# When ten weight chunks are loaded and decoded beside the first block of the feed-forward

## The chip, the cores and the metric

The kernel runs on one core of one Trainium2 chip. Its time is the device time of one execution in microseconds (us); the time of a kernel is the median of the runs shown. A profile is one more execution, recorded by the hardware. Five engines work side by side, each through its own queue in order: TensorE (PE, with its weight loads PEld), VectorE (DVE), ScalarE (ACT), GpSimd (POOL) and SyncE (SP), which here issues all transfers between memory and the chip's buffers.

## The reference

```python
attn = 1.0 / (1.0 + np.exp(-(scale * q @ k.T - log(S))))     # sigmoid attention, per batch and head
x = (attn @ v), heads side by side                           # 3584 tokens x 768
h = x @ w_in                                                 # 768 x 2048
g = h * np.clip(h + 3.0, 0.0, 6.0) / 6.0
out = g @ w_out                                              # 2048 x 768
```

There are 8 batches, 12 heads, 448 positions and 64 numbers a head. The host hands w_in and w_out to the kernel as 64-bit floats, seen there as pairs of 32-bit words.

## The kernel before, in words

The 12 heads of a batch go in 6 pairs, so there are 48 pairs; the 3584 tokens go in 7 tiles of 512. The work has three stages. In the first, pairs 0 to 17 (batches 0 to 2) go through attention on raw inputs (`scores_native`, `av_native`). In the second, the other 30 pairs go through attention on operands split in a high and a low part, mixed with the first half of the feed-forward (`moe_in`) of earlier tiles, that of the last tile behind it; its results g are stored to memory (`gd`). In the third, w_out is applied (`moe_out`).

Between the first and the second stage stands a stretch of pure feed-forward, and the change is there. `moe_in(0)` makes the first token tile: 16 feature blocks of 18 products (L375) each. A block collects in one of two PSUM buffers named ph. When its 18 products are done, ACT (L379) and DVE (L380) turn it into g and so free the buffer; SP then stores g (L382). There are two buffers for g too.

The products need w_in as pairs of a high and a low part in SBUF. It comes in 32 half chunks, numbered n = 0 to 31 and called chunks here; chunks 2k and 2k+1 make the weights of block k. `load_wi(n)` handles one in three parts:

- the load: SP issues a transfer of 384 KB (L362) into a staging buffer;
- the decode (`join_f64`, L58 to L68): one ACT operation (L58), five on DVE (L59, L60, L61, L64, L65), one on POOL (L68, the add);
- the split (`split_f32`): one ACT operation (L73, the high part) and one on POOL (L74, the low part).

The staging buffers are borrowed. From n = 15 on, a chunk with n % 3 = 2 (20, 23, 26, 29) uses one single buffer, called wis here, which is also the buffer into which the q and k of a later pair are loaded (`qkr`, L165). It is free only after the split. The other chunks use two pairs of buffers (wiqh for the raw words, wiql for the result): the raw one is free after the decode on DVE, the other after the split.

`feed(part, i)` calls the parts by a clock of units i. In the first stage a unit is two steps of attention, and units run from 0 to 32. After that a unit is KU products of `moe_in(0)`: unit 33 begins at product 0, unit 34 at product KU, and so on. The list `first` holds the unit of each chunk's load; decode and split follow a fixed number of units later. In a unit, all loads are called first, then decodes, then splits. At product 160 the loads of pair 18 are called (L429), at product 224 its preparation (`prep`, from L181 on), and after 276 products the second stage begins.

In this part the order of instructions on PE, ACT, DVE and POOL is the order of the calls, written out by hand. The order on SP is set by a scheduler from its own estimate of times.

## Time and profile before

| | us |
|---|---|
| median of 3 runs | 1244.57 (1244.23 to 1244.61) |
| profiled execution | 1244.73 |
| its span, first to last instruction | 1242.7 |
| PE busy | 1220.3 |
| DVE busy | 724.2 |
| ACT busy | 519.5 |
| POOL busy | 256.5 |

The first stage ends on PE at 116.13 us from the start of the span, where the first product of `moe_in(0)` begins. The first scores of the second stage begin at 188.78, and the third stage's products at 781.7.

A timeline row reads: start and duration in us, engine, line of the kernel, operation, output<-inputs, the number of instructions merged in the row, and in brackets how long the engine had been idle before it and whose end it waited for. A row of the waits reads: who waited for whom, us in total, how often, the longest. A row of the windows reads: the stretch, its length, busy time and number of instructions of PE, PEld, DVE, ACT and POOL, the granted clock of PE as a share of full speed, the busy share of the transfer engines, and GB/s. A row of a source or tile view gives the shortest, median and longest duration in ns, and the first and last start in us.

### The profile page before, as it was taken

Reading aid. Unit: us, or ns where it says so; the run is one execution under the profiler, and the core shown is the slowest. Engines: PE = TensorE matmul, PEld = TensorE weight load, DVE = VectorE, ACT = ScalarE, POOL = GpSimd, SP = SyncE. Lnnn points to the kernel's source line nnn. Section 1 sums busy time; section 2 is a strip of 40 time slices with the busy share of each in tenths; the row PEclk is TensorE's granted clock in tenths of the full one; section 3 lists DMA queues with packets and bytes.
Section 4 is the critical chain, followed back from the end, with each engine's and each line's share of the span. In section 5 each row is a group of like instructions: output and inputs, shape, how many; then the busy total and the mean of one; then the engine's idle time right before and its main releaser. Section 6 shows DMA issues by size and latency. Waiting matters only on the chain.

```text
span 1242.7 us, 15076 instructions
## 1 busy us (share of the span) xinstructions
PE 1220.3 (98%) x5508; PEld 962.1 (77%) x5508; DVE 724.2 (58%) x1284; ACT 519.5 (42%) x671; POOL 256.5 (21%) x297
## 2 busy tenths in 40 slices
PE   8999699999999999999999999999999999999998
PEld 2334487888888888888888888888888888888887
DVE  4566458888888888988888589873030303030300
ACT  6775234666556665665656535322020202020200
POOL 3343343333333433433333000000000000000000
PEclk9999799999999999999999999999999999999999
DMA  7653335334443334433342177734040404040000
GB/s 248 192 169 113 111 114 155 107 93 113 117 111 107 92 113 117 117 110 89 107 117 80 50 220 285 247 105 152 26 161 26 161 26 161 18 161 26 26 26 25
DMA packets 62570, 142.68 MB, mean 115 GB/s; under 512 B 8224, under 2 KB 29728, under 8 KB 58912
## 3 DMA queue, kind: packets, MB, share of 16 engines
q1 hardware_dynamic: 62496, 141.72, 35.9%
q8 instruction: 43, 0.70, 0.2%
q14 instruction: 31, 0.25, 0.1%
HBM read 101.32 MB, written 40.37 MB: 114 GB/s over the span
## 4 chain that ended last, share of the span: by engine, by line
PE 88%; DVE 1%; issue 1%; POOL 0%; ACT 0%; DVEq 0%; POOLq 0%; ACTq 0%
PE po L539 37%; PE ph L375 36%; PE pv L327 6%; PE sc L270 3%; PE sc L271 3%; PE sc L267 1%; PE sc L314 1%; DVE vbh L191 0%; DVE ql L182 0%; DVE g L380 0%; DVE kbl L204 0%; DVE qp L205 0%; DVE al L277 0%; POOL wis L68 0%; POOL wi L74 0%
## 5 line engine op out<-in xcount | busy, mean ns | idle before, releaser
L375 PE MATMUL ph<-x,wi 128*128 128x512 f32 x2016 | 493.5, 395 | 13.1 <-DVE g L380 13.1
L375 PEld LDWEIGHTS ph<-x,wi 128*128 128x128 f32 x2016 | 379.5, 188 | 95.4 <-DVE g L380 14.3
L539 PE MATMUL po<-gl,woh 128*128 128x512 f32 x672 | 261.4, 389 | 0.0
L539 PE MATMUL po<-gh,woh 128*128 128x512 f32 x672 | 261.4, 389 | 0.0
L539 PE MATMUL po<-gh,wol 128*128 128x512 f32 x672 | 261.4, 389 | 0.0
L546 DVE TENSOR_SCALAR o<-po 128x512 f32<-128x512 f32 x42 | 29.0, 689 | 296.5 <-PE po L539 296.5
L499 ACT CAST gh<-gr 128x2048 fp32r<-128x2048 f32 x28 | 53.6, 1914 | 300.6 <-PE po L539 296.4
L277 DVE TENSOR_TENSOR al<-a,ah 128x896 fp32r<-128x896 f32 x120 | 141.1, 1176 | 50.8 <-ACT a L276 49.8
L539 PEld LDWEIGHTS po<-gh,wol 128*128 128x128 f32 x672 | 126.1, 188 | 26.3
L539 PEld LDWEIGHTS po<-gh,woh 128*128 128x128 f32 x672 | 126.1, 188 | 26.2
L539 PEld LDWEIGHTS po<-gl,woh 128*128 128x128 f32 x672 | 126.1, 188 | 26.1
L275 ACT ACTIVATE ah<-sc,bias_s 128x896 fp32r<-128x896 f32 x120 | 109.9, 915 | 74.6 <-PE sc L271 38.5
L178 POOL TENSOR_TENSOR ka<-qkr,ka 64x448 fp32r<-64x448 f32 x60 | 91.9, 1531 | 132.0 <-issue 118.7
L379 ACT ACTIVATE g<-ph,bias 128x512 f32<-128x512 f32 x112 | 77.2, 690 | 93.6 <-PE ph L375 85.0
L276 ACT ACTIVATE a<-sc,bias_s 128x896 f32<-128x896 f32 x120 | 109.2, 910 | 1.6 <-DVE al L277 0.7
L380 DVE SCALAR_TENSOR_TENSOR g<-g,ph 128x512 f32<-128x512 f32 x112 | 76.2, 680 | 31.6 <-ACT g L379 31.2
L500 DVE TENSOR_TENSOR gl<-gr,gh 128x2048 fp32r<-128x2048 f32 x28 | 64.1, 2289 | 29.1 <-ACT gh L499 29.0
L227 ACT ACTIVATE an<-scn,bias_s 128x896 f32<-128x896 f32 x63 | 60.4, 1007 | 23.9 <-PE scn L225 19.1
L270 PE MATMUL sc<-qh,ka 128*128 128x448 f32 x180 | 65.9, 366 | 0.0
L271 PE MATMUL sc<-ql,ka 128*128 128x448 f32 x180 | 65.9, 366 | 0.0
L188 POOL TENSOR_TENSOR vv<-vr,vv 128x192 fp32r<-128x192 f32 x60 | 35.4, 609 | 143.6 <-issue 141.1
L182 DVE TENSOR_TENSOR ql<-qkr,qh 128x896 fp32r<-128x896 f32 x30 | 57.5, 1918 | 5.1 <-ACT qh L181 2.2
(84 smaller groups left out, 1149.2 us busy)
## 6 DMA issues: line engine op xcount, KB each, us to landing
gd<-g SPq DMA_DIRECT2D x112, 256.0 KB, 2.8
gr<-gd SPq DMA_DIRECT2D x28, 1024.0 KB, 5.6
qkr<-qk SPq DMA_DIRECT2D x120, 224.0 KB, 4.0
ws<-wo SPq DMA_DIRECT2D x24, 512.0 KB, 4.8
outT<-o SPq DMA_DIRECT2D x42, 256.0 KB, 2.0
qkn<-qk SPq DMA_DIRECT2D x18, 448.0 KB, 4.3
wiqh<-wi SPq DMA_DIRECT2D x20, 384.0 KB, 3.2
vr<-vP SPq DMA_DIRECT2D x30, 224.0 KB, 2.5
```

What stands on the lines that cost most here:

```text
L178: nc.gpsimd.tensor_tensor(out=ka[other, j], in0=kr[other, j], in1=ka.bitcast(F32)[other, j], op=ALU.subtract)
L270: nc.tensor.matmul(sc[:, j, :S], ka[:, j, cs], qh[:, j], start=True, stop=False)
L271: nc.tensor.matmul(sc[:, j, :S], ka[:, j, cs], ql[:, j], start=False, stop=True)
L275: nc.scalar.activation(ah[:, js], sc[:, js, :S], AF.Sigmoid, bias=bias_s, scale=scale)
L276: nc.scalar.activation(a[:, js], sc[:, js, :S], AF.Sigmoid, bias=bias_s, scale=scale)
L277: nc.vector.tensor_tensor(out=al[:, js], in0=a[:, js], in1=ah.bitcast(F32)[:, js], op=ALU.subtract)
L327: nc.tensor.matmul(pv[p][j][:, :S], vv[:, j, c, :], a_[:, j], start=(c == 0 and a_ is ah), stop=(c == NC - 1 and a_ is al),)
L375: nc.tensor.matmul(ph, w[:, cc], x, start=(n == 0), stop=(n == 3 * NCC - 1))
L379: i1 = nc.scalar.activation(g, ph, AF.Relu, bias=bias_3, scale=1.0)
L380: i2 = nc.vector.scalar_tensor_tensor(out=g, in0=g, scalar=6.0, in1=ph, op0=ALU.min, op1=ALU.mult)
L500: nc.vector.tensor_tensor(out=gl, in0=gr, in1=gh.bitcast(F32), op=ALU.subtract)
L539: nc.tensor.matmul(po[t, ec], w[:, fc], x[:, u], start=(fc == 0 and n == 0), stop=(fc == NFC - 1 and n == 2))
```

## The change

Two numbers that stand in three places: a unit of the feed-forward is 14 products instead of 16, and chunks 22 to 31 begin one unit later and have three units instead of two between load and decode. Chunks 0 to 21 keep their units.

```diff
-KU = 16
+KU = 14
...
     NU = (NSN + 1) // 2
     first = [n * NU // NWA for n in range(NWA)]
-    first += [NU - 2 + int((n - NWA) * NWU) for n in range(NWA, 2 * NFC)]
+    first += [NU - 1 + int((n - NWA) * NWU) for n in range(NWA, 2 * NFC)]
     way = {}

     def feed(part, i):
         for n in range(2 * NFC):
-            if first[n] + (0, 2, 3)[part] == i:
+            if first[n] + ((0, 2, 3) if n < NWA else (0, 3, 4))[part] == i:
                 if part == 0:
                     way[n] = load_wi(n)
                 next(way[n], None)
```

Worked out from these lines (NU = 32, NWA = 22, NWU = 1.4), load, decode and split are called at these products; u30 to u32 are units of the first stage:

| chunk | before | after |
|---|---|---|
| 20 | u29, u31, u32 | u29, u31, u32 |
| 21 | u30, u32, 0 | u30, u32, 0 |
| 22 | u30, u32, 0 | u31, 14, 28 |
| 23 | u31, 0, 16 | u32, 28, 42 |
| 24 | u32, 16, 32 | 0, 42, 56 |
| 25 | 16, 48, 64 | 28, 70, 84 |
| 26 | 32, 64, 80 | 42, 84, 98 |
| 27 | 64, 96, 112 | 70, 112, 126 |
| 28 | 80, 112, 128 | 84, 126, 140 |
| 29 | 96, 128, 144 | 98, 140, 154 |
| 30 | 128, 160, 176 | 126, 168, 182 |
| 31 | 144, 176, 192 | 140, 182, 196 |

No instruction is added or removed. In the rows below a name such as wis_23_1032 is the buffer of chunk 23 with a serial number, wi_11 is the weights of block 11, and g_0_1 is block 1 of token tile 0.

ACT, from the end of the first stage to the first evacuations, before:

```order
L58 ACTIVATE wiql_21_1009<-wiqh_21_1008 128x384
L58 ACTIVATE wiql_22_1013<-wiqh_22_1012 128x384
L73 CAST wi_10_981<-wis_20_982 128x384
L254 CAST x_1_4_774<-pv_16_1003 128x128
L254 CAST x_1_5_779<-pv_17_1029 128x128
L58 ACTIVATE wis_23_1032<-wis_23_1032 128x384
L73 CAST wi_10_981<-wiql_21_1009 128x384
L73 CAST wi_11_1011<-wiql_22_1013 128x384
L58 ACTIVATE wiql_24_1054<-wiqh_24_1053 128x384
L73 CAST wi_11_1011<-wis_23_1032 128x384
L379 ACTIVATE g_0_0_1124<-ph_0_0_1093,bias_3_117 128x512
```

and of the change:

```order
L58 ACTIVATE wiql_21_1009<-wiqh_21_1008 128x384
L73 CAST wi_10_981<-wis_20_982 128x384
L254 CAST x_1_4_774<-pv_16_1003 128x128
L254 CAST x_1_5_779<-pv_17_1025 128x128
L73 CAST wi_10_981<-wiql_21_1009 128x384
L58 ACTIVATE wiql_22_1030<-wiqh_22_1029 128x384
L379 ACTIVATE g_0_0_1103<-ph_0_0_1077,bias_3_117 128x512
L58 ACTIVATE wis_23_1050<-wis_23_1050 128x384
L73 CAST wi_11_1028<-wiql_22_1030 128x384
L379 ACTIVATE g_0_1_1138<-ph_0_1_1107,bias_3_117 128x512
L58 ACTIVATE wiql_24_1073<-wiqh_24_1072 128x384
```

The decodes of chunks 23 and 24 (L58) and two splits (L73) stood ahead of the first evacuation (L379); now one decode, that of 22, stands between the split of 21 and it, and the decode of 23 lies between the evacuations of blocks 0 and 1.

POOL at the same place, before:

```order
L68 TENSOR_TENSOR wiql_21_1009<-wiql_21_1009 128x384
L68 TENSOR_TENSOR wiql_22_1013<-wiql_22_1013 128x384
L74 TENSOR_TENSOR wi_10_981<-wis_20_982,wi_10_981 128x384
L68 TENSOR_TENSOR wis_23_1032<-wis_23_1032 128x384
L74 TENSOR_TENSOR wi_10_981<-wiql_21_1009,wi_10_981 128x384
```

and of the change:

```order
L68 TENSOR_TENSOR wiql_21_1009<-wiql_21_1009 128x384
L74 TENSOR_TENSOR wi_10_981<-wis_20_982,wi_10_981 128x384
L74 TENSOR_TENSOR wi_10_981<-wiql_21_1009,wi_10_981 128x384
L68 TENSOR_TENSOR wiql_22_1030<-wiql_22_1030 128x384
L68 TENSOR_TENSOR wis_23_1050<-wis_23_1050 128x384
```

The split of chunk 20 (the first L74), which frees the wis buffer for chunk 23, stood behind the adds of 21 and 22; it now stands behind that of 21 alone, and the split of 21 directly behind it.

SP, the loads of chunks and the first stores of g, before:

```order
L362 DMA wiqh_25_1110<-wi 128x768
L362 DMA wis_23_1032<-wi 128x768
L362 DMA wiqh_27_1197<-wi 128x768
L382 DMA gd_0_0_57<-g_0_0_1124 128x512
L362 DMA wis_26_1144<-wi 128x768
L382 DMA gd_0_0_57<-g_0_1_1152 128x512
L362 DMA wiqh_28_1231<-wi 128x768
L382 DMA gd_0_0_57<-g_0_2_1182 128x512
L382 DMA gd_0_0_57<-g_0_3_1217 128x512
```

and of the change:

```order
L362 DMA wis_23_1050<-wi 128x768
L362 DMA wiqh_25_1118<-wi 128x768
L382 DMA gd_0_0_57<-g_0_0_1103 128x512
L382 DMA gd_0_0_57<-g_0_1_1138 128x512
L362 DMA wiqh_27_1196<-wi 128x768
L382 DMA gd_0_0_57<-g_0_2_1173 128x512
L362 DMA wis_26_1150<-wi 128x768
L362 DMA wiqh_28_1226<-wi 128x768
L382 DMA gd_0_0_57<-g_0_3_1208 128x512
```

The load of 23 now stands ahead of that of 25, no load later than 25 stands ahead of the first two stores, and the loads of 26 and 28 stand ahead of the store of block 3.

## The prediction

> **What bounds the kernel now.** I read the page's first two parts, then what TensorE (PE) waited for, then the stretch of that wait in order of time.

> ```profile
> PE 1220.3 (98%) x5508; PEld 962.1 (77%) x5508; DVE 724.2 (58%) x1284; ACT 519.5 (42%) x671; POOL 256.5 (21%) x297
> PEclk9999799999999999999999999999999999999999
> PE ph L375 <- DVE g L380: 13.1, 3, 11.7
> PE scn L225 <- DMA qkn<-qk: 4.9, 2, 4.0
> ```

> PE is busy for 98% of the span, so only its idle time and its slow time can be won. The idle time is nearly one event, 11.7 us behind an evacuation by VectorE (DVE), and the one clock digit below 9 stands in the same slice of 31 us. This is the place:

> ```profile
> 116.13 8.67 PE L375 MATMUL ph<-x,wi 128*128 128x512 f32 x36
> 119.35 1.02 POOL L68 TENSOR_TENSOR wiql<-wiql 128x384 f32<-128x384 f32 x1 [1.94 <-DVE wiql L65]
> 122.31 1.01 POOL L68 TENSOR_TENSOR wiql<-wiql 128x384 f32<-128x384 f32 x1 [1.94 <-DVE wiql L65]
> 123.28 1.01 POOL L74 TENSOR_TENSOR wi<-wis,wi 128x384 fp32r<-128x384 f32 x1
> 124.32 0.33 SPq L362 DMA_DIRECT2D wis<-wi  x1
> 127.67 0.55 ACT L58 ACTIVATE wis<-wis 128x384 f32<-128x384 f32 x1 [9.38 <-DMA wis<-wi]
> 131.66 1.95 POOL L74 TENSOR_TENSOR wi<-wiql,wi 128x384 fp32r<-128x384 f32 x2
> 132.69 0.55 ACT L58 ACTIVATE wiql<-wiqh 128x384 f32<-128x384 f32 x1 [3.66 <-POOL wi L74]
> 133.14 0.49 ACT L73 CAST wi<-wis 128x384 fp32r<-128x384 f32 x1
> 133.55 0.68 ACT L379 ACTIVATE g<-ph,bias 128x512 f32<-128x512 f32 x1
> 135.25 0.56 DVE L65 SCALAR_TENSOR_TENSOR wiql<-wiqh,wiql 128x384 f32<-128x384 uint32 x1
> 135.72 0.68 DVE L380 SCALAR_TENSOR_TENSOR g<-g,ph 128x512 f32<-128x512 f32 x1
> 136.46 52.49 PE L375 MATMUL ph<-x,wi 128*128 128x512 f32 x216 [11.66 <-DVE g L380]
> 188.78 0.36 PE L270 MATMUL sc<-qh,ka 128*128 128x448 f32 x1
> ```

> The 36 products are feature blocks 0 and 1 of token tile 0; block 2 needs the PSUM buffer of block 0, which only two instructions empty, L379 on ScalarE (ACT) and L380 on DVE. L379 is ready when block 0 is done, yet starts at 133.55. Ahead of it in ACT's queue stands the decode of chunk 23 (L58, 127.67), waiting for a transfer issued at 124.32, because its buffer came free only after chunk 20's split on GpSimd (POOL L74, 123.28). That split in turn stood behind the adds of chunks 21 and 22 (119.35, 122.31). After chunk 23 the decode of chunk 24 also waits, for a split (3.66 us). The stall is a queue order, not a lack of engine time. It has a second price:

> ```profile
> 126.50:127.00 0.50, 0.00 (x0) 0.00 (x0) 0.00 (x0) 0.00 (x0) 0.00 (x0) 0.82 0.74 295
> 127.00:127.50 0.50, 0.00 (x0) 0.00 (x0) 0.00 (x0) 0.00 (x0) 0.00 (x0) 0.50 0.04 12
> 140.00:140.50 0.50, 0.50 (x3) 0.37 (x2) 0.44 (x2) 0.00 (x0) 0.00 (x0) 0.53 0.57 147
> 140.50:141.00 0.50, 0.50 (x4) 0.41 (x3) 0.49 (x1) 0.00 (x0) 0.00 (x0) 1.00 0.87 340
> ```

> The column after POOL's is the granted clock: it fell to 0.50 within 126.5 to 127.0 and came back at about 140.5, so PE's first 4 us after the stall ran at half clock.

> **What can be won, in two terms.** The pace of undisturbed products:

> ```profile
> 176.38 0.69 ACT L379 ACTIVATE g<-ph,bias 128x512 f32<-128x512 f32 x1 [2.78 <-PE ph L375]
> 188.98 0.69 ACT L379 ACTIVATE g<-ph,bias 128x512 f32<-128x512 f32 x1 [3.51 <-PE ph L375]
> L375 PE MATMUL ph<-x,wi x36: 392/394/500, 116.1 to 124.4; 128*128 128x512 f32 x36
> ```

> Three blocks of 18 products lie between these two evacuations: 12.60 / 54 = 0.233 us for a product, 4.20 for a block. The last of the 36 began at 124.40, so block 2 could begin at 124.63; it began at 136.46: **11.83 us**. From there 216 products took 188.78 - 136.46 = 52.32 us, where 216 x 0.2333 = 50.40 would do: **1.92 us** for the half clock. Together 13.75 us.

> [...]

> **The change, part by part.** It adds and removes no instruction. Up to the end of the attention on raw inputs nothing moves but chunk 22's decode, so PE should reach 116.13 as before. Then:

> (a) ACT now has, ahead of L379 of block 0: L73 of 20, two copies, L73 of 21, L58 of 22. Chunks 23 and 24 stand behind it. Chunk 22's transfer is the one issued here, long before its use:

> ```profile
> 109.93 0.33 SPq L362 DMA_DIRECT2D wiqh<-wi  x1
> DMA to landing us min/median/max: 2.9/3.2/6.8
> ```

> Even the longest landing of such a transfer, 6.8 us, is over by 116.8. L73 of 21 waits for POOL's add of 21, which ends at 119.35 + 1.02 = 120.37. From the rows 132.69, 133.14 and 133.55 ACT steps by 0.45 and 0.41, so: L73 of 21 at 120.40, L58 of 22 at 120.85, L379 at 121.26 (block 0 is done at about 120.5).

> (b) DVE runs the five operations of 22 ahead of L380. Their cost free of POOL and beside it:

> ```profile
> 128.25 0.36 DVE L59 TENSOR_SCALAR wis<-wis 128x384 f32<-128x384 f32 x1 [4.89 <-ACT wis L58]
> 130.02 0.56 DVE L65 SCALAR_TENSOR_TENSOR wis<-wis 128x384 f32<-128x384 uint32 x1
> 119.52 1.07 DVE L60 TENSOR_SCALAR wiql<-wiql 128x384 int32<-128x384 int32 x1
> ```

> Free, a decode takes 128.25 to 130.58, 2.33 us. Beside POOL's add of 119.35 to 120.37 the 0.36 us operation took 1.07 and ended 0.22 after POOL did. L58 of 22 ends at 121.41. L380 begins 0.09 before the end of the last L65, and PE 0.74 after L380's start (135.72, 136.46). Free: 121.41 + 2.33 - 0.09 + 0.74 = 124.39, ahead of 124.63, no stall. But POOL then does the splits of 20 and 21 back to back (1.95 us for two, row 131.66), from 120.37 to 122.32: L59 is held to 122.54, the other four take 1.97, PE goes at 122.54 + 1.97 - 0.09 + 0.74 = 125.16. That is a stall of 0.5 us. Were a second operation held by 0.7, it would be 1.2. Bounds 0 and 1.2; I take 0.5, since L59 falls inside a POOL operation as the row at 119.52 did.

> (c) Chunk 20's split no longer waits for the add of 22: it runs at 120.37 to 121.34, so chunk 23's transfer is issued at 121.37 instead of 124.32, and its decode, 3.35 us later as before (127.67 - 124.32), at 124.72. Now block 1's evacuation is behind that: L73 of 22 after POOL's add at 125.55, L379 at 125.96. On DVE, L59 of 23, held by that add to about 125.75, then 1.97: L380 at 127.63, PE free to go at 128.37. Block 2 ends at 125.16 + 4.20 = 129.36: **1.0 us of cover**. Behind the waiting L58 of 23 stand L73 of 22 and L379 of block 1; PE alone waits for them. If the cover goes, each us late costs one.

> (d) Later chunks: the same bookkeeping gives covers of 0.8 to 1.8 us for the next blocks if POOL holds DVE once for each decode, and about -0.2 at block 5 if two POOL operations in a row hold it. I take nothing.

> (e) The last chunks end later: chunk 29's split stands at product 154 instead of 144. Its buffer is the one into which q and k of pair 18 are loaded:

> ```profile
> 165.39 1.02 POOL L74 TENSOR_TENSOR wi<-wis,wi 128x384 fp32r<-128x384 f32 x1
> 166.44 0.65 SPq L165 DMA_DIRECT2D qkr<-qk  x1
> L165 SPq DMA_DIRECT2D qkr<-qk x4: 606/612/652, 166.4 to 169.1; - x4
> DMA to landing us min/median/max: 3.9/6.0/6.2
> 181.17 0.93 ACT L181 CAST qh<-qkr 128x896 fp32r<-128x896 f32 x1
> ```

> The four loads waited for that split; the last landed by 169.1 + 6.2 = 175.3 and was first read at 181.17, 5.9 us later. Ten products are 2.3 us, so the cover stays at 3.6: nothing. Weights of block 15 are split at product 196 and used at 270, 17 us later: nothing. SP issues the same transfers as before, in another order (the last rival).

> **Sum:** -11.83 - 1.92 + 0.5 = -13.25. The profiled execution took 1244.73 us (span 1242.7), so 1231.5; the median of the runs shown is 0.16 below that execution, 1244.57, so **1231.3 us**.

> **Rivals.** *The wait moves on to block 1.* Chunk 23's transfer lands late, by the 6.8 us of the row instead of 3.2: 3.6 - 1.0 = 2.6 us of stall, and as the clock fell within 2.2 us of idling, 1.9 more: 1235.8. For it: chunk 23 is the only one with a short cover. Against: the median landing of 3.2. [...]

> *DVE becomes the bound.* A chunk now comes every 1.4 x 14 = 19.6 products, 4.57 us, where it was 22.4 products, 5.23 us. A free decode (2.33) and 0.68 x 4.57 / 4.20 = 0.74 of L380 ask 3.07 of that. If POOL's two operations for a chunk (2.0 us) blocked DVE all their time it would be 5.07, too much by 0.5; over the eight chunks from 24 on 4 us, and 1.2 instead of 0.5 in (b): 1236.0. The rows that decide:

> ```profile
> L60 DVE TENSOR_SCALAR wis<-wis x12: 359/360/1045, 19.8 to 161.4; 128x384 int32<-128x384 int32 x12
> L61 DVE SCALAR_TENSOR_TENSOR wis<-wis x12: 557/558/561, 20.2 to 161.8; 128x384 int32<-128x384 int32 x12
> ```

> In twelve decodes the median L60 is not held at all and no L61 ever is; holds are rare, which speaks against this. [...]

> *The change does not do what it says:* something else holds L379 of block 0 as long as before, 1244.6. For it would speak a wait on ACT that I have overlooked; against it, the transfer of 22 lands seven us early.

> *Slower: a store behind a load.* Stores of g and loads of chunks share SP's queue, and g has two buffers. Now the load of 26, which waits for the split of 23, and that of 28, which waits for the decode of 25, stand ahead of the store of block 3. If they wait over 4.2 us longer than that block's own L380, block 5's L379 has no buffer, and ACT, DVE and PE stop as they did here. One such stall, at 13.75 us, eats the gain; a second one at the load of 29, ahead of the store of block 5, makes it 1244.57 - 13.25 + 27.5 = 1258.8. Against: the decode of 25 stands right ahead of block 3's L380 on DVE, so it ends 0.6 us before it (135.25 + 0.56 and 135.72 + 0.68 show such a pair), and 4.8 us are missing.

> **How the numbers follow.** Forecast 0.80, the wait moved on 0.08, DVE the bound 0.06, no change 0.03, slower 0.03. The forecast's own range is 1230.5 (no stall, and 0.3 for the runs' spread) to 1232.5 (1.2 us of stall, half a us at block 5). Below, 1229.8 if the two later waits on L380 (13.1 - 11.7 = 1.4 us) go as well; above, the first two rivals end at 1236.0. I give 1229.8 to 1236.2. Changes under 0.2%, 2.5 us, cannot be told from none here; the first three cases lie well beyond: faster 0.94, same 0.03, slower 0.03.

> **What would show it.** In the changed profile: PE starts block 2 near 125.2 with idle under 1.2 us; no clock digit below 9 in slice 5; ACT L379 of block 0 near 121.3, before an L58 that reads chunk 23; the transfer of 23 issued near 121.4; the first scores (L270) near 175.5 instead of 188.78. Wrong would be a wait of ACT L379 or PE of over 2 us anywhere up to there, a clock below 1 after it, or PE's start moved from 116.13.

## The result and the profile after

The changed kernel took 1231.68 us (median of 4 runs, 1230.82 to 1232.68), the kernel before 1244.59 beside it (1244.23 to 1244.68). The ratio is 0.9897, with a 95% interval of 0.988 to 0.9914: 12.9 us faster, where 13.25 were predicted. The profiled execution of the changed kernel took 1231.84 us, its span 1230.1, against 1242.7 before.

The page after, its busy times and clock digits, and from the view of waits the row of PE behind the evacuation (sum, number, longest):

```profile
PE 1219.6 (99%) x5508; PEld 961.1 (78%) x5508; DVE 727.4 (59%) x1284; ACT 520.0 (42%) x671; POOL 257.2 (21%) x297
PEclk9999999999999999999999999999999999999999
PE ph L375 <- DVE g L380: 1.8, 3, 1.1
```

The three waits of 13.1 us are now 1.8, the longest 1.1 instead of 11.7, and no slice shows a lower clock. The place itself, in order of time (start, duration, engine, line, and in brackets the idle time before it and what ended it):

```profile
116.68 8.67 PE L375 MATMUL ph<-x,wi 128*128 128x512 f32 x36
119.92 1.02 POOL L68 TENSOR_TENSOR wiql<-wiql 128x384 f32<-128x384 f32 x1 [1.95 <-DVE wiql L65]
120.89 1.02 POOL L74 TENSOR_TENSOR wi<-wis,wi 128x384 fp32r<-128x384 f32 x1
121.85 0.68 ACT L379 ACTIVATE g<-ph,bias 128x512 f32<-128x512 f32 x1
121.86 1.03 POOL L74 TENSOR_TENSOR wi<-wiql,wi 128x384 fp32r<-128x384 f32 x1
121.94 0.33 SPq L362 DMA_DIRECT2D wis<-wi  x1
122.05 1.06 DVE L59 TENSOR_SCALAR wiql<-wiql 128x384 f32<-128x384 f32 x1 [1.08 <-ACT wiql L58]
125.00 0.68 DVE L380 SCALAR_TENSOR_TENSOR g<-g,ph 128x512 f32<-128x512 f32 x1
125.11 0.56 ACT L58 ACTIVATE wis<-wis 128x384 f32<-128x384 f32 x1 [2.58 <-DVE wiql L65]
125.73 14.50 PE L375 MATMUL ph<-x,wi 128*128 128x512 f32 x61 [0.39 <-DVE g L380]
128.28 0.68 DVE L380 SCALAR_TENSOR_TENSOR g<-g,ph 128x512 f32<-128x512 f32 x1
176.23 0.36 PE L270 MATMUL sc<-qh,ka 128*128 128x448 f32 x1
```

L379 of block 0 starts at 121.85, ahead of the decode of chunk 23 (L58, 125.11), where it started at 133.55 behind the decodes of 23 and 24. Block 2 starts 0.39 us after the 36 products instead of 11.66. (The bracket at L58 names L65 of chunk 22, but the transfer of 23, issued at 121.94, landed 3.1 us later, at about 125.0: that is what it waited for.) The first scores stand at 176.23 instead of 188.78, 12.55 us earlier, and the span is 12.6 shorter: whatever was won lies ahead of the second stage, and nothing was given back behind it. On PE the first scores stand behind 252 products, 36 and 216, in both kernels; the 276 named further up are the products called ahead of the second stage, and the last 24 of them run behind these scores.

### The profile page after: what moved, and what is told of

It reads as the page before. It is cut to its first block, busy times and chain, and to the rows that moved or that the text cites. A ratio compares the mean times of both kernels' runs of the same rounds, so it can differ in the third digit from the quotient of the medians.

```text
span 1230.1 us, 15074 instructions
## 1 busy us (share of the span) xinstructions
PE 1219.6 (99%) x5508; PEld 961.1 (78%) x5508; DVE 727.4 (59%) x1284; ACT 520.0 (42%) x671; POOL 257.2 (21%) x297
## 4 chain that ended last, share of the span: by engine, by line
PE 95%; DVE 2%; ACT 1%; DMA 1%; issue 0%; POOL 0%; SPq 0%; DVEq 0%; ACTq 0%; POOLq 0%
PE po L539 37%; PE ph L375 36%; PE pv L327 6%; PE scn L225 3%; PE sc L270 3%; PE sc L271 3%; PE pv L244 3%; PE sc L267 1%; PE sc L314 1%; DMA qkn<-qk 1%; ACT an L227 1%; PE scn L223 1%; PE pv L242 0%; DVE wiql L60 0%; DVE wiql L59 0%
## 5 line engine op out<-in xcount | busy, mean ns | idle before, releaser
L375 PE MATMUL ph<-x,wi 128*128 128x512 f32 x2016 | 491.7, 394 | 1.8 <-DVE g L380 1.8
L375 PEld LDWEIGHTS ph<-x,wi 128*128 128x128 f32 x2016 | 378.2, 188 | 83.6 <-DVE g L380 3.0
L178 POOL TENSOR_TENSOR ka<-qkr,ka 64x448 fp32r<-64x448 f32 x60 | 92.0, 1533 | 127.4 <-issue 114.5
L379 ACT ACTIVATE g<-ph,bias 128x512 f32<-128x512 f32 x112 | 77.2, 689 | 74.7 <-PE ph L375 69.8
L380 DVE SCALAR_TENSOR_TENSOR g<-g,ph 128x512 f32<-128x512 f32 x112 | 76.2, 680 | 18.9 <-ACT g L379 18.6
L270 PE MATMUL sc<-qh,ka 128*128 128x448 f32 x180 | 65.9, 366 | 0.0
L182 DVE TENSOR_TENSOR ql<-qkr,qh 128x896 fp32r<-128x896 f32 x30 | 57.4, 1914 | 5.3 <-ACT qh L181 2.6
```

Of the source, the lines that this page charges most:

```text
L178: nc.gpsimd.tensor_tensor(out=ka[other, j], in0=kr[other, j], in1=ka.bitcast(F32)[other, j], op=ALU.subtract)
L270: nc.tensor.matmul(sc[:, j, :S], ka[:, j, cs], qh[:, j], start=True, stop=False)
L375: nc.tensor.matmul(ph, w[:, cc], x, start=(n == 0), stop=(n == 3 * NCC - 1))
L379: i1 = nc.scalar.activation(g, ph, AF.Relu, bias=bias_3, scale=1.0)
L380: i2 = nc.vector.scalar_tensor_tensor(out=g, in0=g, scalar=6.0, in1=ph, op0=ALU.min, op1=ALU.mult)
```

## The experiments

Twelve runs follow, eleven kernels and the change once more. Each part of the change alone comes first, then the causes named in the prediction, then the last chunks. Line numbers of a kernel with an added line are shifted by one or two; the names of the buffers tell which instruction it is.

**The gap alone.** The kernel before, with only the longer distance between transfer and decode:

```diff
-            if first[n] + (0, 2, 3)[part] == i:
+            if first[n] + ((0, 2, 3) if n < NWA else (0, 3, 4))[part] == i:
```

> From the kernel before, only the third unit between load and decode for chunks 22 to 31 (unit 16 products, load where it was). Decode of 24 goes behind the first evacuation, decodes of 22 and 23 stay ahead of it. Theory (queue order): chunk 20's split on POOL now stands behind the add of 21 alone, so the transfer of 23 is issued near 121.4 and the first evacuation L380 begins near 127.6; PE stands from 124.8 to about 128.4, 3.7 us instead of 11.8; and as the clock fell 1.7 to 2.2 us after PE stopped, it falls here too and costs 1.9: 5.1 us over the changed kernel, about 1236.8. [...] Rival B (the start one unit later is what brings the gain): as before, 1244.6.

Measured: 1236.37 us (1235.83 to 1236.63), ratio 0.9935 (0.992 to 0.995).

```profile
124.96 0.55 ACT L58 ACTIVATE wis<-wis 128x384 f32<-128x384 f32 x1 [3.78 <-DMA wis<-wi]
125.81 0.68 ACT L379 ACTIVATE g<-ph,bias 128x512 f32<-128x512 f32 x1
127.79 0.68 DVE L380 SCALAR_TENSOR_TENSOR g<-g,ph 128x512 f32<-128x512 f32 x1
128.52 11.85 PE L375 MATMUL ph<-x,wi 128*128 128x512 f32 x43 [3.48 <-DVE g L380]
```

Chunk 24 has left the front of ACT's queue, chunk 23 has not: its decode, waiting for the transfer, still stands ahead of L379, and PE waits 3.48 us.

**The later start alone.** The other half of it:

```diff
-    first += [NU - 2 + int((n - NWA) * NWU) for n in range(NWA, 2 * NFC)]
+    first += [NU - 1 + int((n - NWA) * NWU) for n in range(NWA, 2 * NFC)]
```

> From the kernel before, only the start one unit later for chunks 22 to 31 (unit 16, two units to the decode). ACT, DVE and POOL get the same order as with the longer gap alone up to the second evacuation, and the transfer that ends the wait, that of 23, waits for the same split. Theory (queue order): the same stall as there, 3.7 us and a fallen clock, about 1236.8. Rival (what counts is how many units lie between transfer and decode): as before, 1244.6, while the longer gap alone gets most of the gain.

Measured: 1236.36 us (1235.56 to 1237.04), ratio 0.9935 (0.992 to 0.995); PE waits 3.53 us at block 2 and the order on ACT is that of the gap alone. Either half moves chunk 24 and leaves chunk 23: 8 of the 13 us. Both together move the decode two units, and the second unit takes chunk 23 away as well.

**The unit alone.** `KU = 14` in the kernel before.

> From the kernel before, only the unit of 14 products. The decodes of 23 and 24 stand at products 0 and 14, still ahead of the first evacuation at 18, so on ACT and POOL nothing moves there. Theory: the same stall of 11.7 us with a fallen clock, 1244.6. Rival (the denser cadence makes DVE the bound from chunk 25 on): 1246 to 1249. Rival (the unit matters to the gain): 1232 to 1238.

Measured: 1245.09 us (1243.94 to 1245.98), ratio 1.0004 (0.9995 to 1.0014): no difference.

```profile
132.35 0.55 ACT L58 ACTIVATE wiql<-wiqh 128x384 f32<-128x384 f32 x1 [3.66 <-POOL wi L74]
136.12 4.21 PE L375 MATMUL ph<-x,wi 128*128 128x512 f32 x9 [11.52 <-DVE g L380]
```

The decodes of 22 and 23 and the splits of 20 to 22 are called in units of the first stage or at product 0, and these do not move with the number of products in a unit. The decode of 24 moves from product 16 to 14, which is still ahead of the end of block 0 at 18: it waits 3.66 us ahead of L379 as before.

**The queue or the late transfer?** In the kernel before, chunk 23 waited for a transfer that waited for a buffer. Here it gets a buffer of its own, and every decode stays at its place in the queues:

```diff
+        if n == 23:
+            st, ab = (att.tile([P, 2 * w], I32, tag=tag, name=f"wi{tag}_{n}", bufs=1) for tag in ("a", "kn"))
-        if own == 2:
+        elif own == 2:
```

> The kernel before with its order on ACT, DVE and POOL, but chunk 23 is staged in two buffers that pairs 14 and 15 have left, so that its transfer no longer waits for chunk 20's split. Theory (queue order and not the transfer alone): the decode of 23 starts near 118.3 on ACT, but the decode of 24 still waits for the split of 21, which POOL does after the adds of 22 and 23, near 128; L380 of block 0 near 131.0 and PE at about 131.7: a stall of 7.1 us instead of 11.8, with the fallen clock: 1239.9. Rival (the late transfer is the whole cause): no stall left, 1231 to 1232.

Measured: 1240.53 us (1239.03 to 1240.74), ratio 0.9966 (0.9953 to 0.9979).

```profile
117.76 0.57 ACT L58 ACTIVATE wikn<-wia 128x384 f32<-128x384 f32 x1
128.00 0.55 ACT L58 ACTIVATE wiql<-wiqh 128x384 f32<-128x384 f32 x1 [4.54 <-POOL wi L74]
128.85 0.68 ACT L381 ACTIVATE g<-ph,bias 128x512 f32<-128x512 f32 x1
131.76 8.48 PE L377 MATMUL ph<-x,wi 128*128 128x512 f32 x24 [7.38 <-DVE g L382]
```

With its data there, chunk 23 is decoded at 117.76, and the evacuation is now held by the next in the queue: chunk 24, whose buffer waits for a split. PE's stall falls from 11.66 to 7.38 us. So the late transfer was worth 4.3 of the 11.7 us of idling; the rest is that a decode which cannot run yet stands ahead of an evacuation which can. The clock falls here as well: the 216 products to the scores (184.89) took 53.13 us, 2.73 more than 50.40.

**The change without its cover.** Step (c) gave chunk 23 one us of cover. In the changed kernel its transfer is issued twice, which delays its landing:

```diff
-        nc.sync.dma_start(out=st, in_=wi[fc, :, u * w : (u + 1) * w])
+        for _ in range(2 if n == 23 else 1):
+            nc.sync.dma_start(out=st, in_=wi[fc, :, u * w : (u + 1) * w])
```

> The changed kernel with the transfer of chunk 23 issued twice into the same buffer, the second one after the first has landed, so that its decode starts about 3.2 us later. Theory (the second evacuation waits for it with 0.9 us of cover): PE starts block 3 about 2 us late; 1233.7 if the clock holds. The earlier runs let the clock fall and come back on a grid of 3.41 us, after a window in which PE was busy for 41% or less, and not after one of 68%; a 2 us stall inside one window leaves 41 to 44%, so it may fall, which takes 1.7 more: 1235.4. Rival (the transfer of 23 is no longer waited for by PE): 1231.7.

Measured: 1234.74 us (1233.95 to 1235.69), ratio 0.992 (0.9905 to 0.9935).

```profile
124.86 4.47 PE L376 MATMUL ph<-x,wi 128*128 128x512 f32 x18 [0.38 <-DVE g L381]
127.68 0.55 ACT L58 ACTIVATE wis<-wis 128x384 f32<-128x384 f32 x1 [6.04 <-DMA wis<-wi]
131.25 9.05 PE L376 MATMUL ph<-x,wi 128*128 128x512 f32 x31 [1.92 <-DVE g L381]
```

This is the first rival, made to happen: PE waits 1.92 us a block later, and the clock falls too. From 131.25 the 198 products to the first scores (179.10) took 47.85 us, where 198 x 0.2333 = 46.20 would do: 1.65 us more. Together 3.6 us, against 3.3 between the medians of this kernel and of the change beside it (1231.48).

**The change again**, beside the next kernels.

> The changed kernel once more, on the same chip as the three runs beside it: 1231.7, with 0.4 us of idling at block 2 and no fallen clock. Where PE starts its first product (116.1 in the profile of before, 116.7 in that of the change) should vary by some tenths of a us from run to run, if that shift belongs to the executions and not to the change.

Measured: 1231.48 us (1230.78 to 1232.02), ratio 0.9893 (0.9878 to 0.9908), span 1229.8.

**Every decode behind an evacuation.** Decode and split of a chunk are called one product after the end of a block, so that no decode stands between a block's end and its evacuation:

```diff
+    for n in range(NWA, 2 * NFC):
+        for part in range(0 if n > NWA + 1 else 1, 3):
+            late.setdefault(fcm_ * (n - NWA + (-1, 1, 2)[part]) + 1, []).append((part, n))
```

`fcm_` is 18, the products of a block; the loads of pair 18 are called at 166 instead of 160.

> The changed kernel with decodes and splits of chunks 22 to 31 called by product instead of by unit: one decode right behind each block's evacuation, its split behind the next block's, and the loads of pair 18 called at product 166. Theory (the 0.4 us left at block 2 is the decode of 22 ahead of the first evacuation): no wait of PE there, L380 of block 0 about 0.7 us after its L379 starts, 0.5 us less than the changed kernel, 1231.2, which the runs may not tell from it. Rival (the decode behind each evacuation delays the next one through DVE): 1232 to 1234.

Measured: 1230.99 us (1230.44 to 1231.77), ratio 0.9892 (0.9875 to 0.9908). The runs do not tell it from the change; the profile does:

```profile
116.14 59.07 PE L375 MATMUL ph<-x,wi 128*128 128x512 f32 x252
```

All 252 products up to the scores run without a wait: the 0.4 us left at block 2 is gone, and the span is 1228.7 against 1229.8. This is what is still to be had at this place, and it is below what the runs resolve.

**The shifts with the unit of 16.** The changed kernel with `KU = 16`:

> The changed kernel with its unit put back from 14 to 16 products: start one unit later and three units to the decode alone. ACT, DVE and POOL keep the changed order up to the evacuation of block 2. Theory (the two shifts together push the decodes of 23 and 24 behind the first evacuation, the unit does nothing): the same time as the changed kernel, 1231.7, stall at block 2 near 0.5 us. Rival (the denser unit brings part of the gain): 1233 to 1238.

Measured: 1233.94 us (1233.54 to 1234.81), ratio 0.9914 (0.9899 to 0.9929). The expectation was missed by 2.2 us. Block 2 is not the place (PE waits 0.37 there, as in the change); the loss is where the second stage begins:

```profile
168.51 2.38 POOL L74 TENSOR_TENSOR wi<-wiql,wi 128x384 fp32r<-128x384 f32 x2
170.97 3.16 POOL L178 TENSOR_TENSOR ka<-qkr,ka 64x448 fp32r<-64x448 f32 x2
171.18 1.94 DVE L182 TENSOR_TENSOR ql<-qkr,qh 128x896 fp32r<-128x896 f32 x1
178.03 8.67 PE L375 MATMUL ph<-x,wi 128*128 128x512 f32 x36 [0.91 <-DVE g L380]
189.38 3.00 PE L375 MATMUL ph<-x,wi 128*128 128x512 f32 x12 [1.87 <-DVE g L380]
```

and the same five rows in the change again:

```profile
164.14 2.01 POOL L74 TENSOR_TENSOR wi<-wiql,wi 128x384 fp32r<-128x384 f32 x2
169.93 3.02 POOL L178 TENSOR_TENSOR ka<-qkr,ka 64x448 fp32r<-64x448 f32 x2 [3.79 <-issue]
169.63 1.08 DVE L182 TENSOR_TENSOR ql<-qkr,qh 128x896 fp32r<-128x896 f32 x1
177.21 8.66 PE L375 MATMUL ph<-x,wi 128*128 128x512 f32 x36 [0.27 <-DVE g L380]
187.81 3.00 PE L375 MATMUL ph<-x,wi 128*128 128x512 f32 x12 [1.11 <-DVE g L380]
```

With units of 16 the split of chunk 31 is called at product 224, where the preparation of pair 18 is called too. POOL's last two splits then run right ahead of the preparation (168.51), where they were done 3.8 us before it. DVE shows where the loss arises: from the start of L175 to that of L380 of block 12 it needs 8.03 us (169.26 to 177.29) instead of 7.38 (169.09 to 176.47), as much more as PE waits more (0.91 and 0.27). L182 took 1.94 us instead of 1.08; POOL's first L178 had begun 0.2 us ahead of it, where in the change L182 had begun first. Two L203 that ran beside the last split (170.05) took 1.09 us, where in the change the two took 0.42 (174.77). Two causes were left: these splits, or chunk 29's buffer, which comes free later and lets the loads of pair 18 go at 160.68 instead of 156.97. Three kernels were built to part them.

**The shifts for chunks 22 to 26 alone**, unit 16, so that the last chunks stand where they stood before:

```diff
+NWF = 27
-    first += [NU - 1 + int((n - NWA) * NWU) for n in range(NWA, 2 * NFC)]
+    first += [NU - 2 + (n < NWF) + int((n - NWA) * NWU) for n in range(NWA, 2 * NFC)]
-            if first[n] + ((0, 2, 3) if n < NWA else (0, 3, 4))[part] == i:
+            if first[n] + ((0, 3, 4) if NWA <= n < NWF else (0, 2, 3))[part] == i:
```

> The kernel before with unit 16, and the two shifts (start one unit later, three units to the decode) for chunks 22 to 26 alone; chunks 27 to 31 stay where they were, so that the last split is called at product 192 and not at 224, where pair 18 is prepared. Theory (with the unit of 16 the two shifts push the last splits of POOL into the preparation of pair 18; with these chunks left alone that is gone): 1231.7, and PE's two waits behind L380 at the start of the second stage 0.3 and 1.1 us as in the changed kernel. Rival (a denser unit is worth something by itself): 1233.9 as with unit 16.

Measured: 1241.08 us (1240.17 to 1242.2), ratio 0.9972 (0.9962 to 0.9983). Far off both values, because a new stall appears, in block 9:

```profile
151.93 0.33 SPq L363 DMA_DIRECT2D wis<-wi  x1
156.46 0.54 ACT L59 ACTIVATE wis<-wis 128x384 f32<-128x384 f32 x1 [7.65 <-DMA wis<-wi]
160.94 0.68 ACT L380 ACTIVATE g<-ph,bias 128x512 f32<-128x512 f32 x1
162.40 2.07 PE L376 MATMUL ph<-x,wi 128*128 128x512 f32 x4 [7.49 <-DVE g L381]
```

It is the stall of the kernel before at another chunk. Chunk 29 uses the buffer of 26. The split of 26, called late, frees it at 151.9; the decode of 29, called early, waits 7.65 us for the transfer, and behind it in ACT's queue stands an evacuation (160.94). At the second stage PE's two waits are 0.26 and 0.79 us, as the theory had them, but here the splits and the buffer of 29 are both back at their early places, so the kernel does not part the two causes. It shows that the shift must go on to the last chunk that shares the buffer.

**The shifts for chunks 22 to 29**, the same edit with `NWF = 30`:

> As the run with five chunks, but shifted are chunks 22 to 29; only 30 and 31 stay at products 176 and 192 for their splits. Chunk 29's split is called at 176, as late as with unit 16, so the loads of pair 18 are issued near 160.7 as there. Theory A (POOL's last two splits stand ahead of pair 18's preparation and delay it): gone here, 1231.7. Theory B (the buffer of q and k of pair 18 comes free too late): stays, 1233.9.

Measured: 1234.93 us (1234.51 to 1235.25), ratio 0.9923 (0.991 to 0.9935): neither value. Chunks 29 and 30 are now decoded in one unit, PE waits for them (1.70 and 0.60 us), and the loads of pair 18 go later still, at 167.12. POOL's splits were done at 169.05, and POOL's first instruction of the preparation (L179) waited 3.47 us for the loads, to 172.52; PE's two waits at the second stage are 1.22 and 1.24 us. So loads as late as this do cost. For the loads at 160.68 of the kernel with unit 16 it decides nothing.

**Unit 16, chunk 29 in other buffers.** This takes the one cause away and leaves the other:

```diff
+        if n == 29:
+            st, ab = (att.tile([P, 2 * w], I32, tag=tag, name=f"wi{tag}_{n}", bufs=1) for tag in ("a", "kn"))
-        if own == 2:
+        elif own == 2:
```

> The shifts of the change with the unit left at 16 took 1233.94 us, 2.3 more than the change, all of it lost where the second stage begins (PE waits of 0.91 and 1.87 us instead of 0.27 and 1.11). This kernel is that one, but chunk 29 lands in two other buffers (tags a and kn), so that the loads of q and k of pair 18 no longer wait for its split and are issued some 8 us earlier; the two splits of chunks 30 and 31 on POOL still stand directly ahead of the preparation of pair 18. Theory A (POOL's splits ahead of the preparation cost the 2.3 us): 1233.9, and the two waits stay near 0.9 and 1.9. Theory B (the late buffer of chunk 29 costs them, step (e) of the prediction): 1231.7, and the waits go back to about 0.3 and 1.1.

Measured: 1233.72 us (1233.16 to 1235.04), ratio 0.9908 (0.9892 to 0.9925), the value of theory A.

```profile
144.43 3.08 SPq L165 DMA_DIRECT2D qkr<-qk  x4
167.61 2.38 POOL L74 TENSOR_TENSOR wi<-wiql,wi 128x384 fp32r<-128x384 f32 x2
177.12 8.66 PE L377 MATMUL ph<-x,wi 128*128 128x512 f32 x36 [0.91 <-DVE g L382]
188.49 4.61 PE L377 MATMUL ph<-x,wi 128*128 128x512 f32 x12 [1.89 <-DVE g L382]
```

The loads of pair 18 now go at 144.43, 16 us earlier, and the two waits stay at 0.91 and 1.89. The late buffer is not the cause of the 2.3 us. (In this profiled execution the clock fell behind the second wait: its 12 products took 4.61 us instead of 3.00. It is the longest of the four runs; the others lie at 1233.16 to 1234.02.) What is left is the end of the decode work, the two splits on POOL right ahead of the preparation; that they alone do it, no run here separates from the decodes of 30 and 31, which come later with them, and from the order on DVE, which is not quite the same: in both kernels with unit 16 the two L203 of pair 18 stand ahead of L182 (170.05 and 169.16), in the change behind it.

**The preparation earlier.** The kernel with every decode behind an evacuation, and the preparation of pair 18 called at product 206 instead of 224, to take the two waits of the second stage away:

```diff
-NPP = 224
+NPP = 206
```

> The kernel with each decode right behind an evacuation, and pair 18's preparation called at product 206 instead of 224, one block earlier. Theory (the 0.27 and 0.9 us that PE still waits behind L380 at the start of the second stage come from the preparation's fourteen DVE operations ahead of block 12's L380): both go, 1230.0. Rival (pair 19's operations wait for transfers and take that place, or the preparation now waits for the transfers of pair 18): 1231.0 or more.

Measured: 1233.28 us (1232.6 to 1235.22), ratio 0.9914 (0.99 to 0.9927): a median 2.3 us above that with 224, with intervals that overlap (0.9875 to 0.9908 there).

```profile
160.85 2.61 SPq L165 DMA_DIRECT2D qkr<-qk  x4
167.59 0.94 ACT L181 CAST qh<-qkr 128x896 fp32r<-128x896 f32 x1 [3.26 <-DMA qkr<-qk]
174.15 6.24 PE L375 MATMUL ph<-x,wi 128*128 128x512 f32 x19 [2.83 <-DVE g L380]
```

Called so early, the preparation waits on ACT for its own loads (3.26 us), and one wait of 2.83 us on PE takes the place of two of 0.27 and 0.92. In this execution the clock fell behind that wait, too: 19 products took 6.24 us, where 18 x 0.2333 and the 0.39 of the last make 4.59. It is the mistake of the kernel before made anew: an instruction placed ahead of its data.

## Why the prediction was right, point by point

**What bounds the kernel** was read rightly: a queue order. The own buffer for chunk 23 splits the 11.7 us into 4.3 for a late transfer and 7.4 that stay with the transfer in time, which the prediction had told as one chain.

**The two terms and the 0.5 us.** From PE's first product to block 2 the prediction had 125.16 - 116.13 = 9.03 us; it took 125.73 - 116.68 = 9.05. From there to the first scores it had 50.40 us at full clock; it took 176.23 - 125.73 = 50.50. So the three terms of the sum are right to 0.12 us together. (By the prediction's measure, from 0.23 us after the start of the last of the 36, the stall is 0.55 where 0.53 was worked out; the view's 0.39 counts from the end of that product.) The instants named in (a) to (c) stand 0.54 to 0.66 us later than predicted, which is in the main the 0.55 by which PE's own start is late: L379 at 121.85 for 121.26, the transfer of 23 at 121.94 for 121.37, the two L380 at 125.00 and 128.28 for 124.42 and 127.63. The one exception is L58 of chunk 23, 125.11 for 124.72: it began 3.17 us after the transfer was issued, not 3.35.

**Step (b)'s hold** came as written: L59 of chunk 22 began beside POOL's second split and took 1.06 us instead of 0.36, ending 0.22 after it. **Step (c)'s cover:** L380 of block 1 began at 128.28, so PE could go at 129.0, and block 2 ended at 125.73 + 4.20 = 129.93: 0.9 us, 1.0 predicted. That it is as thin as said, and what it costs when it is gone, the doubled transfer showed. **Step (d):** no wait up to the scores.

**Step (e), "nothing",** is right for the change and too short in its working. It looked at the buffer of chunk 29 alone. The kernels with the unit of 16 show that the place has a second limit, the end of the decode work against the preparation of pair 18, and that it decides: two products more in each unit put the change 2.3 us back. The unit of 14, which alone does nothing, is what makes the two shifts free of charge. The prediction had no term for this part of the change at all.

**What was wrong** is the start: "PE should reach 116.13 as before". It reached 116.68, 0.55 us later, and this is the gap between the predicted 13.25 and the 12.6 of the spans. The start is not the change's: over the fourteen profiles it lies between 115.65 and 116.68, the changed kernel itself, profiled again, has 116.41, and the kernel with the doubled transfer, whose order is the same up to there, 115.82. The 0.3 us that the range kept for the spread of runs was meant for the end; the sum took an instant of one execution as fixed. A trifle beside it: 1231.3 less the 1.4 us of the two later waits is 1229.9, not the 1229.8 given as the lower bound.

**The rivals.** DVE became no bound: no wait on L380 up to the scores but the 0.39. One reason given against that rival was weaker than it looked, though. That "no L61 ever is" held says little, since in the traces before and after no L61 runs beside a POOL instruction; what did run beside one, unheld at 0.68 us, is L380, which takes one of its two inputs from PSUM. Another line that, like L61, takes both inputs from SBUF did meet POOL, and was held: in the kernel with unit 16, L182 began 0.2 us behind POOL's L178 and took 1.94 us, where in the change, begun 0.3 us ahead of it, it took 1.08. What L61 itself does beside POOL was not shown. The store behind a load did not happen.

**The clock** as a price was right in kind: 1.92 us before, and nothing once the stall was 0.39. The reason given, a fall within 2.2 us of idling, was only what one execution showed; what the runs show stands in the last section.

## What to carry to other kernels

Here an instruction that waited for its data held everything behind it on its engine (on ACT the decode of chunk 23 waited for 9.38 us, that of 24 for 3.66, and PE behind them for 11.66), so what is placed ahead of a PSUM evacuation must have its data by then, and a step that shares a buffer must be moved together with every later user of that buffer. Half of such a move may win most of the time or open the same stall further on; follow the new order to its end, to the next stage's first work, before calling it free. Price a stall of PE by its idle time and by the clock that may fall behind it, which cost another 1.61 to 2.73 us in these runs.

## What the hardware showed beyond this

```profile
129.50:130.00 0.50, 0.50 (x2) 0.36 (x2) 0.50 (x1) 0.50 (x2) 0.50 (x1) 0.55 1.01 381
132.50:133.00 0.50, 0.50 (x3) 0.35 (x2) 0.00 (x0) 0.00 (x0) 0.50 (x1) 0.53 0.32 37
```

and of the one with the doubled transfer:

```profile
131.50:132.00 0.50, 0.50 (x3) 0.34 (x3) 0.47 (x2) 0.24 (x1) 0.50 (x2) 0.73 0.00 0
135.00:135.50 0.50, 0.50 (x4) 0.42 (x3) 0.20 (x1) 0.00 (x0) 0.50 (x1) 0.86 0.00 0
```

A mean of 0.55 in a stretch that starts at 1.00 puts the fall at 129.55, a mean of 0.53 the return at 132.97: 3.42 us. With the doubled transfer it is 131.73 and 135.14: 3.41. In the kernel before, by the rows of the prediction, 126.82 and 140.47: 13.65, four times 3.41. In the first two PE had been at work again, for 1.0 and 0.5 us, when the clock fell: the fall can come after the stall. From the end of PE's work to the fall it was 2.0 us before, 4.5 with the gap alone and 2.4 with the doubled transfer.

The grid is there from the start. A trace also records the moment at which the clock first came to full speed: in the kernel before at 7.355 us, and from there to the fall at 126.822 it is 119.47 us, 35 times 3.413; in the changed kernel at 10.483, and to its one fall, at 1229.041, 1 us before the end of the span, it is 1218.56, 357 times 3.413. So the grid can be laid through the kernel with unit 16 alone, which has no fall here. Its first 16 products took 6.32 us from 4.20, those of the changed kernel 6.33 from 4.29, 6.19 of them up to full speed; that makes an estimated 10.37 for full speed, and 52 windows on stands about 187.86.

That would tell why the same stall brings a fall in one execution and not in the other. The second wait is 1.87 us with unit 16 alone and 1.89 with chunk 29 in other buffers as well, at the same place of the program; behind the one the 12 products took 3.00 us, behind the other 4.61. The two windows of the grid at the wait without a fall, and then the one at the wait with it:

```profile
184.44:187.86 3.42, 3.08 (x14) 2.25 (x12) 3.33 (x7) 1.94 (x4) 2.48 (x4) 1.00 0.00 0
187.86:191.27 3.41, 1.89 (x8) 1.60 (x9) 3.41 (x10) 1.60 (x2) 0.00 (x0) 1.00 0.62 158
185.10:188.51 3.41, 1.52 (x8) 0.98 (x7) 3.32 (x7) 2.57 (x3) 1.47 (x4) 1.00 0.23 60
```

The wait without a fall, 187.51 to 189.38, lies across a border of the grid, and PE was still busy for 1.89 of the 3.41 us behind it, 55%. The wait with a fall, 186.60 to 188.49, lies within one window, of which PE was busy for 1.52, 45%. The other traces agree: the window ahead of a fall was one with PE busy for 30% (gap alone), 41% (before), 44% (doubled transfer) and at most these 45%. In the traces of before and of the change every window at full clock that no fall followed had PE busy for 66% or more, and with unit 16 the one of 55% was followed by none. Where between 45 and 55% the border lies, no run here shows. The waits of 0.36 to 0.39 us at block 2 brought no fall. The price beside the idle time was 1.61 to 2.73 us, near half of the time for which PE then worked at half clock: 1.66 with the gap alone (3.41 us of it), 1.92 before (4.0), 2.73 with chunk 23 in its own buffer (5.8).

**PE's arrival at a fixed point varied by a us between executions,** 115.65 to 116.68 us after the span's start; two profiles of the changed kernel differ by 0.27. A sum over a few us that starts from such an instant carries that much.
